# A three-stage attention and mixture-of-experts kernel: a search step's counts moved to ScalarE, a planner with other lengths, and the last expert's chunks in reverse order

## The chip, the cores and the metric

One core of a Trainium2 chip runs the whole kernel in one launch. The metric is device microseconds for that launch, the median of three runs. PE, DVE, ACT, POOL and SP below are the engines TensorE, VectorE, ScalarE, GpSimd and SyncE.

## What is computed

An attention over 2 x 5056 tokens with 256 channels feeds a first mixture of experts, whose result feeds a second one. The change touches the second alone: 8 experts, each takes the 1264 tokens (`cap`) with the largest logits that no earlier entry has taken, and each token is computed by its one expert as two matrix products with a ReLU between.

```python
def _moe2_ref(x, w_gate, w1, w2):
    N, D, E = 10112, 256, 8
    cap = N // E
    logits = x @ w_gate
    ...                       # sorted logits, largest first; token -> expert while the expert has room
    for e in range(E):
        mask = assigned == e
        h = np.maximum(x[mask] @ w1[e], 0.0)     # 256 -> 1024
        out[mask] = h @ w2[e]                    # 1024 -> 256
```

## The kernel before

The attention runs to about 290 us, the first mixture to about 780 us, and the second from there to the end. Only the second stage's instructions stand in another order after the change.

**Routing.** Before expert p can start, its tokens are picked. The threshold is found by a radix search over a 128x688 array of 16-bit keys, first over the high halves (`hk`), then over the low halves (`lk`): `search`, L365 to L404, eight steps each, for seven of the eight experts, so 14 searches and 112 steps. A step compares all keys with three candidates. One of them is always counted on ACT (`sign`, L376, a Sign activation with an accumulated sum), one always on DVE (`count`, L373, a comparison with an accumulated sum); the third goes to ACT in every second step (`i % 2`) and to DVE in the others. `fold` (L384) sums the three counts over the partitions by a tiny matmul on PE, `digit` (L389) and `next_` (L393) on DVE make the next candidates, and the next step starts. ACT and DVE also do the ReLU of the experts (`hh`, L786 on ACT; `hl`, L794, the remainder, on DVE), and PE does their matmuls, so the small instructions of the search are threaded between those.

**Tokens.** `slots` (L602 on) turns the mask into row numbers: `SEL` matmuls (L639), then DVE. `load` (L665) gathers the expert's 1264 rows from DRAM into `xi` with ten indirect DMAs issued by POOL (L682, 128 rows each, the last 112), and copies the token numbers out as `ti` (L686, L687). `split` (L694) transposes the rows on PE (L735) into `xh` (L738, ACT) and `xl` (L743, DVE), chunk by chunk. `CH` is three chunks: 256, 512 and 496 rows (2, 4 and 4 tiles of 128).

**The expert.** `ffn` (L754) runs 20 units per expert. A unit is `F1` (L773, 12 matmuls into `pb`) and, three units later, `F2` (L814, 12 matmuls into `py`). At a chunk's end ACT copies pairs of tiles of `py` to `yo` (L832; L834 and L835 where the last tile is short), and POOL scatters them, one tile at a time, to the output by an indirect DMA (L840). There are two `yo` buffers and one `xi` buffer.

**What sets the order.** `Order` (L215) is a planner that runs when the program is built. Every operation is posted with an assumed duration and its dependencies; the planner repeatedly issues the operation with the earliest start minus a bonus, which the table `BONUS` gives by engine, kind of operation and expert number (0, 1, 2, 3 or more). That fixes the sequence of instructions on each engine; nothing is reordered on the chip.

Of the kernel before, what the change touches and what calls it, by code (L numbers as in the profile page):

```python
# [57 lines left out]
BONUS = {  # L58
    "ACT": (-1.03, -1.15, -1.39, -1.15),
    "ACTC": (-0.13, -0.68, -1.07, -1.07),  # L60
    "ACTH": (-1.73, -0.92, -1.14, -1.04),
    "ACTS": (1.24, -1.09, -0.67, -1.18),
    "ACTW": (-0.91, -1.77, -2.02, -1.86),
    "ACTX": (-0.83, -0.69, -0.38, -0.76),
    "DVE": (2.14, 0.09, 0.17, 0.07),
    "DVEC": (0.18, 0.11, 0.22, 0.09),
    "DVEH": (0.05, 0.14, 0.02, 1.58),
    "DVES": (-0.01, 0.13, 0.03, 0.07),
    "DVEW": (-0.02, 0.05, 0.58, -0.04),
    "DVEX": (4.11, 0.14, 0.02, 1.78),  # L70
    "PE": (-0.22, -0.01, 0.11, 0.1),
    "PEP": (-0.22, -0.14, 0.01, 0.18),
    "PES": (-0.42, 0.06, -0.01, 0.18),
    "PEX": (-0.12, -0.15, 6.41, 0.11),
    "POOL": (1.04, 3.11, 0.41, 1.07),
    "POOLG": (2.72, -1.84, -6.0, 1.07),
    "POOLW": (4.84, 2.33, 1.93, 5.0),
    "SP": (0.14, 3.17, -1.95, 3.19),
}
# [200 lines left out]
def second(ctx, tc, k, l2, code, keyd, ys, w12, w22, out, ident, onesf, trib, ie, rp, r2, late):  # L280
# [84 lines left out]
    def search(x, thr, after, thr_op):  # L365
# [3 lines left out]
        for i in range(ND - 1, -1, -1):  # L369
# [15 lines left out]

            def digit(f=slice(i % 2, i % 2 + 3)):
                j = col("dj", 3)
                s.d = col("dd")
                V.scalar_tensor_tensor(j, s.pe[:, f], 0.0, thr()[:, f], op0=ALU.add, op1=ALU.is_ge, accum_out=s.d)  # L389
# [6 lines left out]

            c3 = A(0.87, lambda c=sign: c(2), *dep, b="C")
            c1 = A(0.87, lambda c=sign: c(3), *dep, b="C") if i % 2 else W(0.86, lambda c=count: c(0), *dep, b="C")
            c2 = W(0.86, lambda c=count: c(1), *dep, b="C")
            ob = W(0.07, base, *dep, c2) if i else None  # L400
# [6 lines left out]
    def route(p_, st, p2):  # L407
# [37 lines left out]
        ont = W(0.07, lambda: above(hf, ss), od, on, b="C")  # L445
        onh = A(0.86, lambda: S.activation(junk2, hk, AF.Sign, bias=hf.nth, accum_out=nh), ont, b="C")
        olk = W(0.85, lambda: V.scalar_tensor_tensor(lk, hk, hf.th, kp[:, 1, :], op0=ALU.is_equal, op1=ALU.mult), oth, b="C")
        z = Slot()
# [76 lines left out]

        onl = A(0.86, nlow, ont, b="C")
        z3 = Slot()
# [137 lines left out]
    def load(st, pv, puts):  # L665
# [23 lines left out]
        for r in range(NR):  # L689
            st.g.append(PL(1.2, lambda r=r: rows(r), st.sis[r], st.g[-1] if r else None, *(pv.xs if pv and not r else []),  # L690
                           *([pv.tok] if pv else [(q, 2.3) for q in puts]), b="G"))
        st.tok = PL(0.3, toks, (st.g[-1], 2.3))

    def split(st, p2, prev):  # L694
# [18 lines left out]
        for j, (h, l, r) in enumerate((("w1h", "w1l", "w1r"), ("w2h", "w2l", "w2r"))):  # L713
            for i in range(4):
                f = (slice(None), slice(2 * i, 2 * i + 2), slice(None)) if j else (slice(None), slice(None), slice(i * 256, i * 256 + 256))
                o = A(0.52, lambda h=h, r=r, f=f, x=(not j and not i): hi(h, r, f, x), (st.w, 7.4 if j else 4.3), wp[0][0] if wp else None,
                      *([p2.last] if p2 else []), b="W")
                o2 = W(0.6, lambda l=l, h=h, r=r, f=f: lo(l, h, r, f), o, b="W")
                wp.append((o, o2))
        st.w1s, st.w2s = wp[:4], wp[4:]  # L720
        st.ws = [q for o in wp for q in o]
        st.xc, st.xs = {}, []
        for ci, (t0, nt, n) in enumerate(CH):
            for c in range(2):
                s, z = State(), Slot()
                ss = slice(t0 * P, t0 * P + n)

                def tr(c=c, s=s, t0=t0, nt=nt, n=n):
                    if t0 == 0 and c == 0:
                        st.xh = pxi.tile([P, 2, NR * P], F32R, name="xh")  # L730
                        st.xl = pxi.tile([P, 2, NR * P], F32R, name="xl")
                    s.pt = qh.tile([P, 512], F32, name="pb")
                    for t in range(nt):
                        m = min(P, n - t * P)
                        T.transpose(s.pt[:, t * P:t * P + m], st.xi[:m, t0 + t, c * P:(c + 1) * P], ident[:m, :m])  # L735
# [4 lines left out]
                def xlo(i, c=c, s=s, t0=t0, nt=nt, n=n):  # L740
# [3 lines left out]

                ot = M(0.107 * nt, tr, (st.g[t0 + nt - 1], 2.3), *([st.xs[-1]] if st.xs else [p2.last] if p2 else []), b="X",
                       take=[("pb", z)])
# [7 lines left out]
    def ffn(st, prev):  # L754
# [46 lines left out]
        def f2(x, y, ci_, t0, nt, n, nch, u):  # L801
# [22 lines left out]
            if u == 8 // nch - 1:  # L824
                for h in range(nt // 2):
# [21 lines left out]
                    for t in range(2):  # L847
                        st.out = PL(1.27, lambda t=2 * h + t, put=put: put(t), oy, st.tok, free=[zy])

        for ci_, (t0, nt, n) in enumerate(CH):  # L850
            nch = 4 // nt
            y = State()
            y.py, y.z = {}, [Slot() for _ in range(nt // 2)]
            for u in range(8 // nch):
                x = State()
                x.zh = Slot()
                units.append((x, y, ci_, t0, nt, n, nch, u))
# [31 lines left out]
    for p_ in range(E):  # L889
# [3 lines left out]
        slots(p_, z, sts[-1] if p_ else None, sts[-2] if p_ > 1 else None)  # L893
        sts.append(z)
        load(z, sts[-2] if p_ else None, () if p_ else puts)
        split(z, sts[-3] if p_ > 1 else None, prev)
# [1179 lines left out]
```

## Time and profile before

| | |
|---|---|
| median of 3 runs | 1435.3 us (1434.08 to 1438.9) |
| the profiled execution's own time | 1436.2 us |
| its span, first to last instruction | 1434.5 us |
| mean granted TensorE clock | 0.951 of full speed |
| PE busy | 1301.4 us, 91% |
| DVE busy | 1094.7 us, 76% |
| ACT busy | 797.6 us, 56% |
| POOL busy | 316.4 us, 22% |

The profile is a record of one execution. Its page gives busy time by engine, the span in 40 equal slices (each digit the busy share in tenths), and the chain of work that ended last. The views used below are the slices and the chain, a table of busy time per stretch of 20 us, the list of waits by releaser, and single instructions in order of time. "another core or an unknown queue" and "remote" mean that the record shows no instruction whose end matches the release; with one core this stands where an engine waited for a signal although the record has the sender done.

### The profile page before, as it was taken

What the parts mean: (1) busy time and instruction counts of PE and PEld (TensorE: products, weight loads), DVE (VectorE), ACT (ScalarE), POOL (GpSimd) and SP (SyncE); (2) the same over time, 40 slices, a digit from 0 to 9 for tenths busy, and PEclk for the clock granted to TensorE, in tenths of its full rate; (3) what the DMA queues carried; (4) which work ended last, traced back from release to release, by engine and by line L of the source; (5) the groups of instructions that cost most, each with busy time, mean ns of one, the idle gap of its engine ahead of it and who ended that gap; (6) DMA issues with size and microseconds to landing.
All of it is one profiled execution on the core that took longest, in us unless ns stands there. A gap on an engine that the chain in (4) does not pass through costs nothing.

```text
span 1434.5 us, 25591 instructions
## 1 busy us (share of the span) xinstructions
PE 1301.4 (91%) x8726; PEld 1169.3 (82%) x8726; DVE 1094.7 (76%) x3720; ACT 797.6 (56%) x1640; POOL 316.4 (22%) x419
## 2 busy tenths in 40 slices
PE   8986858799999999999999987979898999897997
PEld 7886747489988988989987986878888889796897
DVE  8985434698899989798997768989898889685221
ACT  5563424456665666475774657655666666553221
POOL 7634554200000000000000003231423232324312
PEclk9998978799999999999999998989999999998999
DMA  8894531476595959477660981212121212123100
GB/s 292 278 311 150 179 118 61 143 249 192 161 330 170 310 180 293 148 252 248 223 183 16 399 321 50 84 48 78 55 89 45 89 52 85 48 94 107 44 22 30
DMA packets 136226, 223.26 MB, mean 156 GB/s; under 512 B 22016, under 2 KB 99840, under 8 KB 134048
## 3 DMA queue, kind: packets, MB, share of 16 engines
q1 hardware_dynamic: 120256, 186.44, 39.0%
q0 software_dynamic: 11520, 31.73, 6.6%
q10 hardware_dynamic: 4320, 3.46, 0.7%
q8 instruction: 69, 1.13, 0.3%
q14 instruction: 61, 0.50, 0.1%
HBM read 170.18 MB, written 51.41 MB: 154 GB/s over the span
## 4 chain that ended last, share of the span: by engine, by line
PE 71%; DVE 15%; another core or an unknown queue 4%; ACT 4%; issue 3%; DMA 2%; POOL 1%; SPq 0%; ACTq 0%; DVEq 0%; POOLq 0%
PE py L814 15%; PE pb L773 14%; PE pb L1824 12%; PE py L1855 10%; PE pd L2020 4%; PE px L1322 3%; PE ps L1088 2%; PE px L1326 2%; DVE w2l L1793 2%; DVE junk L373 1%; PE pt L1301 1%; DVE hl L1837 1%; PE pt L1770 1%; PE pt L1461 1%
## 5 line engine op out<-in xcount | busy, mean ns | idle before, releaser
L1824 PE MATMUL pb<-xhl,w1h 128*128 128x512 f32 (+1 forms) x800 | 211.1, 351 | 1.7 <-ACT w1h L1787 1.2
L814 PE MATMUL py<-w2l,hh 128*128 128x256 f32 (+1 forms) x640 | 183.9, 287 | 0.0
L814 PE MATMUL py<-w2h,hl 128*128 128x256 f32 (+1 forms) x640 | 183.2, 286 | 0.8 <-issue 0.8
L786 ACT ACTIVATE hh<-pb 128x512 fp32r<-128x512 f32 (+1 forms) x160 | 93.8, 589 | 157.9 <-PE pb L773 112.5
L814 PE MATMUL py<-w2h,hh 128*128 128x256 f32 (+1 forms) x600 | 174.9, 292 | 3.3 <-issue 3.3
L794 DVE SCALAR_TENSOR_TENSOR hl<-pb,hh 128x512 fp32r<-128x512 f32 (+1 forms) x160 | 108.4, 678 | 75.9 <-ACT hh L786 68.6
L1824 PEld LDWEIGHTS pb<-xhl,w1h 128*128 128x128 f32 x800 | 134.1, 190 | 19.2 <-ACT w1h L1787 1.6
L840 POOL DMA_INDIRECT out_dram<-yo,ti x80 | 79.4, 992 | 309.0 <-ACT yo L832 245.2
L1836 ACT ACTIVATE hh<-pb 128x512 fp32r<-128x512 f32 x148 | 88.6, 599 | 104.8 <-PE pb L1824 79.7
L773 PE MATMUL pb<-xh,w1h 128*128 128x256 f32 (+2 forms) x384 | 140.8, 367 | 4.2 <-DVE hl L794 4.2
L1855 PE MATMUL py<-w2h,hh 128*128 128x264 f32 x496 | 143.6, 290 | 0.1
L1855 PE MATMUL py<-w2h,hl 128*128 128x264 f32 x496 | 142.0, 287 | 0.3 <-DVE hl L1837 0.2
L1855 PE MATMUL py<-w2l,hh 128*128 128x264 f32 x496 | 142.2, 287 | 0.0
L773 PE MATMUL pb<-xl,w1h 128*128 128x256 f32 (+2 forms) x384 | 141.1, 368 | 0.4 <-issue 0.2
L773 PE MATMUL pb<-xh,w1l 128*128 128x256 f32 (+2 forms) x384 | 140.1, 365 | 0.0
L1824 PE MATMUL pb<-xhl,w1l 128*128 128x512 f32 (+1 forms) x400 | 138.2, 346 | 0.0
L2034 POOL COPY yo<-xm 128x16 f32<-128x16 f32 x6 | 2.2, 368 | 578.3 <-DVE g L1880 491.6
L814 PEld LDWEIGHTS py<-w2l,hh 128*128 128x128 f32 (+1 forms) x640 | 122.3, 191 | 6.0 <-issue 1.8
L814 PEld LDWEIGHTS py<-w2h,hl 128*128 128x128 f32 (+1 forms) x640 | 122.2, 191 | 2.0 <-issue 0.3
L814 PEld LDWEIGHTS py<-w2h,hh 128*128 128x128 f32 (+1 forms) x600 | 114.7, 191 | 6.2 <-issue 2.4
L1837 DVE SCALAR_TENSOR_TENSOR hl<-pb,hh 128x512 fp32r<-128x512 f32 x148 | 101.3, 684 | 19.1 <-ACT hh L1836 18.3
L682 POOL DMA_INDIRECT xi<-y_scr,si x80 | 80.7, 1009 | 90.1 <-issue 18.6
(521 smaller groups left out, 3714.4 us busy)
## 6 DMA issues: line engine op xcount, KB each, us to landing
w2r<-in_moe_w_dram SPq DMA_DIRECT2D x45, 1024.0 KB
w1r<-in_moe_w_dram SPq DMA_DIRECT2D x41, 1024.0 KB
vt<-in_v_dram SPq DMA_DIRECT2D x18, 512.0 KB
qt<-in_q_dram SPq DMA_DIRECT2D x17, 512.0 KB
kt<-in_k_dram SPq DMA_DIRECT2D x17, 512.0 KB
h_scr<-hh SPq DMA_DIRECT2D x32, 256.0 KB
h_scr<-hl SPq DMA_DIRECT2D x32, 256.0 KB
xi<-xe_scr SPq DMA_DIRECT2D x14, 536.0 KB
```

Of the source, the lines that this page charges most:

```text
L682: G.indirect_dma_start(out=st.xi[:n, r, :], out_offset=None, in_=ys, in_offset=bass.IndirectOffsetOnAxis(ap=st.si[:n, r:r + 1], axis=0))
L773: T.matmul(x.pb[:, ci, :n], a[:, c, fc * P:fc * P + P], b_[:, c, xs_], start=(c == 0 and i == 0), stop=(c == 1 and i == 2))
L786: S.activation(x.hh[:, :, :n], x.pb[:, :, :n], AF.Relu)
L794: V.scalar_tensor_tensor(x.hl[f], x.pb[f], 0.0, x.hh[f].bitcast(F32), op0=ALU.max, op1=ALU.subtract)
L814: T.matmul(py[:m_, t % 2, :], a[:, ci, t * P:t * P + m_], b_[:, fc, :], start=False, stop=(fc == 7 and i == 2 and t % 2 == 1))
L840: s_ = G.indirect_dma_start(out=out, out_offset=bass.IndirectOffsetOnAxis(ap=st.ti[:m_, t0 + t:t0 + t + 1], axis=0), in_=q.yo[:m_, t % 2, ...
L1322: T.matmul(w.px[:np_, :D + 2 * E], h.vh[:, cc, tt, :np_], r[:, cc, :], start=(i == 0), stop=False)
L1824: T.matmul(o, a[:, c, ws], xhl[:, c, h, :], start=(i == 0), stop=(i == 5))
L1836: S.activation(hh, pb, AF.Relu)
L1837: V.scalar_tensor_tensor(hl, pb, 0.0, hh.bitcast(F32), op0=ALU.max, op1=ALU.subtract)
L1855: T.matmul(py[t][:, :width], a[:, ci, ts_], b_[:, fc, :width], start=(fc == 0 and i == 0), stop=(fc == 7 and i == 2))
L2020: T.matmul(py[t][:, :D], a[:, ts_], b_[:, fc, :D], start=(fc == 0 and i == 0), stop=(fc == 7 and i == 2))
```

## The change

Three edits. First, in `search` the third candidate goes to ACT where `i % 4` is not zero, six steps of eight in place of four. Second, the planner's assumed lengths: a sign 1.0 us (was 0.87), a count 0.9 (0.86), a gather's issue 1.4 (1.2) and its landing 3.0 (2.3), a scatter's issue 1.42 (1.27), the casts of the weights 5.0 and 8.0 us after their load is issued (4.3 and 7.4), and another `BONUS` table. Third, the last expert runs its chunks in reverse: 496, 512, 256 rows.

```diff
 BONUS = {
-    "ACTS": (1.24, -1.09, -0.67, -1.18),
+    "ACTS": (0.14, -0.62, 1.75, -0.54),
...
-    "POOLG": (2.72, -1.84, -6.0, 1.07),
+    "POOLG": (2.41, -2.03, -5.16, -0.42),
...
-            def digit(f=slice(i % 2, i % 2 + 3)):
+            def digit(f=slice(i % 4 > 0, (i % 4 > 0) + 3)):
...
-            c3 = A(0.87, lambda c=sign: c(2), *dep, b="C")
-            c1 = A(0.87, lambda c=sign: c(3), *dep, b="C") if i % 2 else W(0.86, lambda c=count: c(0), *dep, b="C")
-            c2 = W(0.86, lambda c=count: c(1), *dep, b="C")
+            c3 = A(1.0, lambda c=sign: c(2), *dep, b="C")
+            c1 = A(1.0, lambda c=sign: c(3), *dep, b="C") if i % 4 else W(0.9, lambda c=count: c(0), *dep, b="C")
+            c2 = W(0.9, lambda c=count: c(1), *dep, b="C")
...
-            st.g.append(PL(1.2, lambda r=r: rows(r), st.sis[r], st.g[-1] if r else None, *(pv.xs if pv and not r else []),
+            st.g.append(PL(1.4, lambda r=r: rows(r), st.sis[r], st.g[-1] if r else None, *(pv.xs if pv and not r else []),
...
-        st.tok = PL(0.3, toks, (st.g[-1], 2.3))
+        st.tok = PL(0.4, toks, (st.g[-1], 3.0))
...
-                o = A(0.52, lambda h=h, r=r, f=f, x=(not j and not i): hi(h, r, f, x), (st.w, 7.4 if j else 4.3), wp[0][0] if wp else None,
+                o = A(0.52, lambda h=h, r=r, f=f, x=(not j and not i): hi(h, r, f, x), (st.w, 8.0 if j else 5.0), wp[0][0] if wp else None,
...
-        for ci, (t0, nt, n) in enumerate(CH):
+        for ci, (t0, nt, n) in st.ch:
...
-                    if t0 == 0 and c == 0:
+                    if ci == st.ch[0][0] and c == 0:
...
-                ot = M(0.107 * nt, tr, (st.g[t0 + nt - 1], 2.3), *([st.xs[-1]] if st.xs else [p2.last] if p2 else []), b="X",
+                ot = M(0.107 * nt, tr, (st.g[t0 + nt - 1], 3.0), *([st.xs[-1]] if st.xs else [p2.last] if p2 else []), b="X",
...
-                        st.out = PL(1.27, lambda t=2 * h + t, put=put: put(t), oy, st.tok, free=[zy])
+                        st.out = PL(1.42, lambda t=2 * h + t, put=put: put(t), oy, st.tok, free=[zy])
...
-        for ci_, (t0, nt, n) in enumerate(CH):
+        for ci_, (t0, nt, n) in st.ch:
...
+        z.ch = list(enumerate(CH))[::-1 if p_ == E - 1 else 1]
```

The order moves in many places of the second stage. Three of them follow.

POOL, the gathers (L682) of expert 6 and the scatters (L840, each with a small MEMSET ahead of it) of expert 5 around them, before:

```order
L682 DMA xi<-y_scr,si 128x260 x7
L839 MEMSET gap 128x1
L840 DMA out_dram<-yo,ti 10112x256
L682 DMA xi<-y_scr,si 128x260
L839 MEMSET gap 128x1
L840 DMA out_dram<-yo,ti 10112x256
L839 MEMSET gap 128x1
L840 DMA out_dram<-yo,ti 10112x256
L839 MEMSET gap 128x1
L840 DMA out_dram<-yo,ti 10112x256
L682 DMA xi<-y_scr,si 128x260
L682 DMA xi<-y_scr,si 112x260
```

The same place after:

```order
L682 DMA xi<-y_scr,si 128x260 x9
L682 DMA xi<-y_scr,si 112x260
L839 MEMSET gap 128x1
L840 DMA out_dram<-yo,ti 10112x256
L839 MEMSET gap 128x1
L840 DMA out_dram<-yo,ti 10112x256
```

The ten gathers of expert 6 stand in one piece, and the scatters that stood between them stand behind them. For expert 5 the order was the same as for expert 6 and becomes the same; for expert 7 one scatter stood after the fourth and one after the fifth gather, and now none stands between. Experts 1 and 3 had their ten gathers in one piece before and have it still; expert 4 had it, and now has one scatter after its second gather; expert 2 had four scatters ahead of its last gather, and has them after its seventh.

ACT, one search over the high halves, the fifth of seven, for expert 4 (`cnt` is the counts of a step, two buffers in turn, so a row "x2" on one `cnt` is two candidates of one step; `dr` and `w1h` belong to the next tokens and weights), before:

```order
L376 ACTIVATE junk_10962,cnt_10964<-hk,k_kk 128x688 x2
L629 CAST dr_10968<-pc 128x87
L786 ACTIVATE hh<-pb 128x496
L376 ACTIVATE junk_10962,cnt_10963<-hk,cand 128x688
L832 COPY yo<-py 128x512 x2
L786 ACTIVATE hh<-pb 128x496
L376 ACTIVATE junk_10962,cnt_10964<-hk,cand 128x688 x2
L707 CAST w1h<-w1r 128x2x256
L786 ACTIVATE hh<-pb 128x496
L376 ACTIVATE junk_10962,cnt_10963<-hk,cand 128x688
```

The same search after:

```order
L376 ACTIVATE junk_10962,cnt_10964<-hk,k_kk 128x688 x2
L786 ACTIVATE hh<-pb 128x496
L707 CAST w1h<-w1r 128x2x256
L376 ACTIVATE junk_10962,cnt_10963<-hk,cand 128x688 x2
L786 ACTIVATE hh<-pb 128x496
L832 COPY yo<-py 128x512
L376 ACTIVATE junk_10962,cnt_10964<-hk,cand 128x688 x2
L832 COPY yo<-py 128x512
L786 ACTIVATE hh<-pb 128x496
L738 CAST xh<-pb 128x256
L376 ACTIVATE junk_10962,cnt_10963<-hk,cand 128x688
```

The second step, which counted one candidate on ACT, counts two; the fourth still counts one.

ACT, the end of the program, the last expert's ReLUs (`hh`) and output copies (`yo`), before:

```order
L786 ACTIVATE hh<-pb 128x512 x7
L832 COPY yo<-py 128x512
L786 ACTIVATE hh<-pb 128x512 x5
L786 ACTIVATE hh<-pb 128x496 x3
L832 COPY yo<-py 128x512 x2
L786 ACTIVATE hh<-pb 128x496 x5
L832 COPY yo<-py 128x512
L834 COPY yo<-py 128x256
L835 COPY yo<-py 112x256
```

The same place after:

```order
L786 ACTIVATE hh<-pb 128x496 x8
L786 ACTIVATE hh<-pb 128x512 x3
L832 COPY yo<-py 128x512
L834 COPY yo<-py 128x256
L835 COPY yo<-py 112x256
L786 ACTIVATE hh<-pb 128x512 x8
L832 COPY yo<-py 128x512 x2
L786 ACTIVATE hh<-pb 128x512
L832 COPY yo<-py 128x512
```

Behind the last ReLU three copies with four tiles stood, and now one with two tiles stands there.

## Rows read from the trace of the kernel before

**Rows 1.** the page: engines and granted clock in 40 slices, then the chain by engine

```profile
PE   8986858799999999999999987979898999897997
...
PEclk9998978799999999999999998989999999998999
...
PE 71%; DVE 15%; another core or an unknown queue 4%; ACT 4%; issue 3%; DMA 2%; POOL 1%; SPq 0%; ACTq 0%; DVEq 0%; POOLq 0%
```

**Rows 2.** stretches: length, busy PE, PEld, DVE, ACT, POOL; clock, DMA share, GB/s

```profile
880.00:900.00 20.00, 17.73 (x113) 15.47 (x114) 19.60 (x70) 13.68 (x29) 3.38 (x8) 1.00 0.08 26
...
920.00:940.00 20.00, 14.96 (x109) 12.36 (x107) 16.29 (x59) 13.56 (x29) 9.39 (x12) 0.98 0.42 137
...
1020.00:1040.00 20.00, 18.91 (x140) 17.71 (x141) 19.25 (x71) 15.58 (x33) 5.79 (x11) 1.00 0.09 32
...
1080.00:1100.00 20.00, 17.91 (x143) 17.33 (x144) 17.73 (x49) 15.57 (x33) 11.09 (x19) 1.00 0.20 65
...
1140.00:1160.00 20.00, 20.00 (x159) 19.09 (x158) 18.53 (x60) 15.46 (x34) 12.18 (x15) 1.00 0.29 81
...
1220.00:1240.00 20.00, 13.29 (x80) 11.70 (x81) 10.16 (x27) 7.55 (x16) 10.89 (x17) 0.83 0.23 71
...
1280.00:1300.00 20.00, 18.09 (x139) 16.40 (x137) 13.79 (x39) 8.25 (x18) 11.71 (x15) 0.94 0.72 250
1300.00:1320.00 20.00, 13.29 (x84) 11.99 (x83) 12.43 (x28) 9.01 (x17) 3.26 (x5) 0.72 0.08 26
1320.00:1340.00 20.00, 16.53 (x105) 14.47 (x104) 6.02 (x12) 5.29 (x11) 12.15 (x17) 1.00 0.28 80
```

**Rows 3.** the chain from 780 us: start, us, what held it

```profile
935.35 2.69 another core or an unknown queue
...
1014.96 2.90 another core or an unknown queue
...
1084.90 1.77 another core or an unknown queue
...
1226.79 7.15 another core or an unknown queue
...
1292.72 3.71 another core or an unknown queue
1298.26 7.38 another core or an unknown queue
...
1328.09 9.23 another core or an unknown queue
```

**Rows 4.** POOL in order of time, expert 5's gathers: start, us, idle before

```profile
1212.46 1.42 POOL L682 DMA_INDIRECT xi<-y_scr,si  x1 [8.50 <-PE pe L384]
...
1223.64 0.99 POOL L840 DMA_INDIRECT out_dram<-yo,ti  x1 [0.19 <-issue]
...
1231.30 0.95 POOL L682 DMA_INDIRECT xi<-y_scr,si  x1 [0.31 <-issue]
```

**Rows 5.** lines 373 and 376: durations min/median/max in ns

```profile
L373 DVE TENSOR_SCALAR_CACHE_REDUCE junk<-hk,cand x77: 911/924/931, 791.1 to 1241.6; 128x688 bf16<-128x688 uint16 x77
L373 DVE DVE_READ_ACCUMULATOR junk<-hk,cand x77: 75/82/85, 791.9 to 1242.4; 128x1 fp32r x77
...
L376 ACT ACTIVATE junk<-hk,cand x70: 857/869/882, 791.1 to 1240.3; 128x688 bf16<-128x688 uint16 x70
L376 ACT ACTIVATION_READ_ACCUMULATOR junk<-hk,cand x70: 185/187/206, 791.9 to 1241.1; 128x1 fp32r x70
```

**Rows 6.** waits of the second stage: us in total, times, longest

```profile
PE pe L384 <- ACT junk L376: 13.2, 9, 3.3
```

**Rows 7.** the end, in order of time

```profile
1425.84 0.28 PE L814 MATMUL py<-w2h,hl 128*112 128x256 f32 x1
...
1426.31 0.96 POOL L840 DMA_INDIRECT out_dram<-yo,ti  x1 [13.48 <-ACT yo L832]
...
1430.10 0.94 POOL L840 DMA_INDIRECT out_dram<-yo,ti  x1 [0.19 <-issue]
```

## What the change will do to the time

> **What bounds the kernel now.** I read the 40 slices first, then the chain, then the second stage in stretches of 20 us, then single instructions of the poor stretches. The slices say that PE is the bound: nines nearly everywhere in the second half [rows 1], where the change works, and the chain is PE for 71% of the span. A time is to be had only where PE is not at nine, or is at nine with a lower clock. The stretches show where that is. In the middle of an expert PE is busy 20.00 of 20 us, even through the whole gather of expert 4 (1140 to 1160). Around the gathers of the last three experts it is not: expert 5 has 13.29 of 20 (1220 to 1240), expert 6 has 18.09 and 13.29 (1280 to 1320), expert 7 has 16.53 (1320 to 1340) [rows 2]. Together that is 6.71 + 1.91 + 6.71 + 3.47 = 18.8 us without a matmul, and in two of the stretches the granted clock is 0.83 and 0.72, so that part of them ran at 1.2 in place of 2.4 GHz. Earlier experts lose less: expert 1 lost 5.04 (920 to 940), expert 3 lost 2.09 (1080 to 1100), expert 4 nothing.
>
> The chain says the same in another way. Behind 780 us it names seven stretches in which the engine that was last had no sender in the record: 2.69, 2.90 and 1.77 us for experts 1, 2 and 3, then 7.15, 3.71, 7.38 and 9.23, which is 27.5 us, inside the gathers of experts 5, 6 and 7 [rows 3]. What differs there is the order on POOL. Expert 5's ten gathers began at 1212.46, the last at 1231.30, with scatters such as that of 1223.64 between them [rows 4]; experts 1, 3 and 4 had ten in a piece. A tile's transpose waits for its gather, and PE runs its queue in order: a gather that comes late holds not only the new expert's transposes but every matmul behind them.
>
> **Part 1, the gathers in one piece.** For experts 5 and 6 the new order takes four scatters from between the gathers, for expert 7 two. An issue of this kind takes (1430.10 - 1426.31) / 3 = 1.26 us [rows 7], so the last gather starts 5.1 us sooner (2.5 in expert 7), and expert 5's window falls from 18.8 us to about 13.7. On PE the first F1 of experts 5, 6 and 7 also stands later against the older work, because the planner now reckons 1.4 us per gather and 3.0 for its landing. The upper bound of the gain takes the chain's 27.5 us and leaves each of the three a clean expert's share, (2.69 + 1.77 + 0) / 3 = 1.5: 23 us. The middle value takes the time without a matmul, 18.8 us, and leaves the clean mean of (5.04 + 2.09 + 0) / 3 = 2.4 each: 11.6 us. The other end is 0. I take **-15**, between the two ways of counting and nearer to the idle time, since the chain also counts time in which PE's records are busy, while the low clock, which the idle time doesn't count, goes with the stall. The scatters that are put behind the gathers cost nothing as long as the two `yo` buffers come free in time; a chunk of four tiles is 8 units' worth of work, and two buffers wait at most for the ten gathers, 12.6 us.
>
> The trace has the low clock only behind stalls: 1.00 in the stretch 1140 to 1160 without a gap, 0.83 and 0.72 in those with 6.7 us of them [rows 2]. The Trainium skill, "TensorE: Matmul & The Clock Gate", section "HAM oscillation — how this bites in real kernels", says that waits between bursts of matmuls put the clock back to half, so that a wait is paid a second time by what follows it. The trace agrees with 0.72. By that rule the gain would be the idle time and the clock's share, nearer to the upper bound.
>
> **Part 2, the third candidate on ACT.** In each of 14 searches two of eight steps change: 28 candidates. A count takes 0.924 + 0.082 = 1.006 us of DVE, a sign 0.869 + 0.187 = 1.056 us of ACT [rows 5]. DVE loses 28 x 1.006 = 28.2 us of work, 4 us per expert, and ACT gets 28 x 1.056 = 29.6. The length of a step hardly changes: two counts in a row (2.01) were its longest part where two candidates were DVE's, two signs (2.11) are it now, 0.1 us x 28 = 2.8 us of search, which has no room to matter unless the search itself is last. On the path is only what DVE held PE up: DVE is full in 880 to 900 (19.60 of 20) and 1020 to 1040 (19.25), where PE lost 2.27 and 1.09 us [rows 2]. So at best -3.4; I take **-3**. ACT stays under 16 of 20 us in the transitions shown (15.57, 15.58) [rows 2], so its average has room; its queue is in order, though, and a sign of 0.87 us ahead of a ReLU can delay an F2. What is to be seen of that today is PE waiting for a fold whose sign was late: 13.2 us in 9 places, 1.47 each [rows 6]. The planner took two signs for 1.74 us, 0.37 less than they last, and now takes 2.0, 0.11 less, so each fold is put later and waits less. With 84 two-sign steps in place of 56 the wait would rise by half, +6.6; with the truer lengths it could fall by as much. I take **0**, with -6 and +13 as the ends (+13 is worked out under the second rival).
>
> The Trainium skill, "ScalarE: Activation LUTs", section "Rules for kernel authors", speaks against this part: simple arithmetic belongs on VectorE, up to about three times faster. Here the two differ by 5% (1.006 against 1.056), so the rule's gain is not there; by it the move would cost ACT much more than DVE gets back.
>
> **Part 3, the short chunk last.** Behind the last matmul, which ends at 1425.84 + 0.28 = 1426.1, four scatters follow from 1426.31, the last at 1430.10, and the span ends 4.4 us later [rows 7]. With two tiles at the end there are two scatters: 2 x 1.26 = 2.5 us sooner. The first of them no longer overlaps PE's last matmuls, since its copy now waits for the very last one: 0.5 us back. **-2**; the scatters of the chunk before it have the last chunk's four units of matmuls as cover.
>
> **The sum.** 1436.2 (the profiled execution, 0.9 above the median) - 15 - 3 + 0 - 2 = 1416.2; against the median 1435.3 that is **1415**. The first stages keep their order and their time.
>
> **Rivals.** First: the stalls belong to ten gathers as such, not to what stands between them. For it: expert 1 lost 5.04 us with ten in a piece, about as much as expert 5; the late experts also load weights (DMA at 250 GB/s in 1280 to 1300, the place of expert 6's gathers [rows 2]), which the change doesn't move. Against it: expert 4 lost nothing. Then only parts 2 and 3 are left: 1435.3 - 3 - 2 = 1430.
>
> Second, slower: the sign becomes the end of the step. The place is the fold on PE, behind which all F1 and F2 queue; the price is 1.47 us for each fold that is reached before its sign is read out. If 9 of the 28 new two-sign steps wait so, that is +13, and a search that ends later makes the mask, the row numbers and the gathers late, so that part 1 brings nothing: 1435.3 + 13 - 3 - 2 = 1443. With part 1 gone it decides from the fourth such step on (4 x 1.47 = 5.9 against 5); with part 1 in place only from the fourteenth. For it: PE waits for late signs already. Against it: the longer assumed sign, by which each fold is put later.
>
> Third: the last expert gives its gain back. Its first chunk is now of tiles 6 to 9, so no F1 can start before the last of ten gathers, where two were enough: 8 x 1.26 = 10.1 us later, against three units of F2 in hand (36 matmuls, 4.5 us at the 159 in 20 us of the stretch 1140 to 1160 [rows 2]). Its 5 us of part 1 go, and 10.1 - 4.5 = 5.6 are added: 1426.
>
> Fourth: the low clock goes with the stalls and the upper bound of part 1 is reached, and folds wait less: 1435.3 - 23 - 3.4 - 2.5 - 1 = 1405.
>
> **How the numbers follow.** My forecast, 1408 to 1420, has 42%; the third rival's 1426 has 14%, the fourth 8%, the first 16%, the second, with what else could make it slower, 20%. The predicted time is 1415. What a measurement can tell from no change is 0.3%, 4.3 us: the limits are 1431.0 and 1439.6. Faster takes the forecast, the third, the fourth and half of the first: 72%. Within takes the other half and the mild end of the second: 11%. Slower: 17%. The range leaves out the second rival's middle and upper end and the far end of the fourth: 1403 to 1438.
>
> **What would show it.** Right: the three stretches of the chain without a sender in experts 5 to 7 are gone or under 3 us each, the stretches there show PE above 18 of 20 with the clock at 1.00, the gathers of experts 5 to 7 span about 14 us, DVE's full stretches fall under 19, and two scatters stand behind the last matmul. Wrong on part 1: stalls of 7 us stay with gathers in one piece. Wrong on part 2: the fold's waits for a sign grow past 13.2 us, or new waits of `hl` and F2 for a late ReLU appear. Wrong on part 3: a wait of PE at the start of the last expert that is longer than 9.23 us.

## The result and the profile after

The changed kernel took 1451.0 us (median of 4 runs, 1443.7 to 1454.8) against 1434.7 us of the kernel before (4 runs): a ratio of 1.0102, interval 1.0057 to 1.0146. It is slower by 1.0%, where 1415 us, 1.4% faster, was predicted.

The jobs (a job is a set of runs made together on one chip) fell into two kinds, whatever the kernel and not tied to a chip: in *late* jobs, as in the one of the prediction, the kernel before took 1434 to 1438 us and some of PE's results reached the other engines late, and in *prompt* jobs it took 1344 to 1349 us and no such result is in any trace. Kernels are compared with the kernel before of their own job, except where the difference between the kinds is the subject.

The page of the changed kernel, its slices of PE and clock, and its chain by engine (the answer to [rows 1]):

```profile
PE   8988767699999999999999979798869889898998
...
PEclk9999878799999999999999989899999989999999
...
PE 70%; DVE 14%; issue 4%; ACT 4%; another core or an unknown queue 4%; DMA 4%; POOL 1%; SPq 0%; POOLq 0%; ACTq 0%; DVEq 0%
```

The weak slices have moved forward: sixes and sevens stand now where experts 0 to 4 change over. Stretches of 20 us of the changed kernel (length, busy PE, PEld, DVE, ACT, POOL, clock, DMA share, GB/s), the answer to [rows 2]:

```profile
880.00:900.00 20.00, 19.86 (x131) 17.95 (x131) 15.87 (x61) 15.67 (x34) 6.47 (x11) 1.00 0.13 40
...
920.00:940.00 20.00, 10.92 (x63) 10.00 (x62) 11.02 (x32) 9.79 (x21) 5.63 (x9) 0.74 0.15 43
...
1080.00:1100.00 20.00, 13.74 (x88) 13.20 (x89) 13.63 (x42) 13.43 (x27) 2.07 (x4) 0.74 0.05 19
...
1140.00:1160.00 20.00, 13.42 (x89) 11.38 (x87) 8.63 (x31) 8.79 (x20) 13.91 (x18) 0.90 0.42 126
1160.00:1180.00 20.00, 15.82 (x102) 14.62 (x103) 14.64 (x46) 14.02 (x30) 1.01 (x5) 0.76 0.02 7
...
1220.00:1240.00 20.00, 17.70 (x117) 14.76 (x116) 13.55 (x48) 12.46 (x27) 13.94 (x17) 1.00 0.45 138
1240.00:1260.00 20.00, 16.79 (x120) 15.90 (x119) 15.98 (x46) 14.83 (x32) 4.85 (x12) 0.91 0.09 33
...
1300.00:1320.00 20.00, 14.25 (x101) 13.43 (x100) 11.38 (x31) 5.91 (x13) 9.92 (x11) 0.83 0.50 158
1320.00:1340.00 20.00, 19.90 (x144) 18.29 (x142) 14.12 (x28) 11.07 (x22) 13.15 (x17) 1.00 0.31 95
1340.00:1360.00 20.00, 17.23 (x104) 15.59 (x105) 6.57 (x11) 6.32 (x12) 4.21 (x10) 0.91 0.09 31
```

The second stage as a whole, from its first matmul of one group (the marks of the last table under Experiments) to the end, in the same columns, before and then after:

```profile
791.90:1434.50 642.60, 580.71 (x4026) 531.50 (x4024) 461.92 (x1548) 353.32 (x728) 173.99 (x260) 0.96 0.28 96
...
781.50:1448.70 667.20, 590.52 (x4026) 539.69 (x4024) 442.51 (x1489) 378.85 (x782) 169.37 (x260) 0.94 0.26 92
```

PE does the same 4026 matmuls. The stage is 24.6 us longer: PE waits 14.8 us more (76.7 against 61.9), and its records are 9.8 us longer, at a mean granted clock of 0.94 against 0.96. The part ahead of the mark, which the change leaves alone, was 10.4 us shorter in this one profile, so the spans differ by 14.2 us only. Expert 1 (920 to 940) lost 9.1 us, experts 3 and 4 lost 6.3 and 6.6 + 4.2 us in the stretches shown, and the clock fell to 0.74 to 0.90 with them. In all stretches from 900 to 1180, which hold experts 1 to 4, PE waits 42.5 us where it waited 19.2; from 1220 to 1360, which hold experts 5 to 7, it waits 14.8 where it waited 18.8. DVE is relieved, but by 19.4 us and not by the 28.2 worked out: the records of a count, of its read and of the next instruction overlap, so adding their durations says too much. The stretch 880 to 900 has DVE at 15.87 of 20 where it was at 19.60. The chain's stretches without a sender in the record (the answer to [rows 3]: start, us):

```profile
921.30 6.63 another core or an unknown queue
...
1020.68 3.19 another core or an unknown queue
...
1072.89 10.60 another core or an unknown queue
...
1150.41 12.22 another core or an unknown queue
...
1308.74 5.59 another core or an unknown queue
```

They are 38.2 us where they were 34.8, and have gone from experts 5 and 7 to experts 1, 3 and 4. What such a stretch is shows in the single instructions of expert 4's (start, us, engine, line, in brackets the idle time ahead and its releaser):

```profile
1149.49 0.27 PE L384 MATMUL pe<-cnt,k_blk 128*128 128x4 f32 x1 [0.34 <-issue]
...
1152.71 0.58 ACT L786 ACTIVATE hh<-pb 128x496 fp32r<-128x496 f32 x1 [3.28 <-PE pb L773]
...
1155.02 0.28 PE L814 MATMUL py<-w2h,hl 128*112 128x256 f32 x1
...
1162.65 0.16 DVE L389 SCALAR_TENSOR_TENSOR dj<-pe,k_thr 128x3 f32<-128x3 f32 x1 [12.24 <-remote]
...
1163.81 0.75 PE L773 MATMUL pb<-xh,w1h 128*128 128x496 f32 x1 [8.52 <-DVE hl L794]
```

PE's fold of a search step stands in the record at 1149.49, and PE goes on through matmuls queued behind it until 1155.3. DVE, which needs that fold, gets it at 1162.65, 12.9 us after it ended. Not every result is late: ACT's ReLU at 1152.71 starts 0.9 us behind the matmuls that it reads. Once it has the fold, DVE makes `hl`, and PE, out of work for 8.5 us, starts again. Among the ten gathers of expert 4 a single scatter stood, after the second; those of experts 1 and 3, with stretches of 6.63 and 10.60 us, stood in one piece. The waits of the second stage (who waits, for whom, us in total, times, longest), DVE's for a fold before and after, then the answer to [rows 6]:

```profile
DVE dj L389 <- remote: 14.6, 4, 7.2
...
DVE dj L389 <- remote: 32.6, 4, 12.2
...
PE pe L384 <- ACT junk L376: 17.4, 9, 7.9
```

The longest of these nine waits for a sign, 7.9 us, follows a late result: DVE got a fold late at 928.66, so the next step's sign was late too, and the next fold waited for it.

```profile
928.66 0.16 DVE L389 SCALAR_TENSOR_TENSOR dj<-pe,k_thr 128x3 f32<-128x3 f32 x1 [6.50 <-remote]
...
931.38 0.37 PE L384 MATMUL pe<-cnt,k_blk 128*128 128x4 f32 x1 [7.92 <-ACT junk L376]
```

The other eight make 9.5 us. Of the nine waits of before, 13.2 us in all, the longest, 3.3 us, follows a late result too, and the other eight make 9.9.

### The profile page after: what moved, and what is told of

Its sections match the earlier page's. It is cut to its first block, busy times and chain, and to the rows that moved or that the text cites. A ratio compares the mean times of both kernels' runs of the same rounds, so it can differ in the third digit from the quotient of the medians.

```text
span 1448.7 us, 25584 instructions
## 1 busy us (share of the span) xinstructions
PE 1303.2 (90%) x8726; PEld 1170.8 (81%) x8726; DVE 1075.6 (74%) x3664; ACT 825.3 (57%) x1696; POOL 312.9 (22%) x419
## 4 chain that ended last, share of the span: by engine, by line
PE 70%; DVE 14%; issue 4%; ACT 4%; another core or an unknown queue 4%; DMA 4%; POOL 1%; SPq 0%; POOLq 0%; ACTq 0%; DVEq 0%
PE pb L773 14%; PE py L814 14%; PE pb L1826 13%; PE py L1857 10%; PE px L1324 3%; PE pd L2022 3%; PE px L1328 2%; PE pt L1303 1%; ACT junk L376 1%; PE pb L735 1%; DVE junk L373 1%; DVE w2l L1795 1%; PE pt L1772 1%; PE ps L1090 1%
## 5 line engine op out<-in xcount | busy, mean ns | idle before, releaser
L814 PE MATMUL py<-w2h,hl 128*128 128x256 f32 (+1 forms) x640 | 188.3, 294 | 2.2 <-issue 1.1
L814 PE MATMUL py<-w2l,hh 128*128 128x256 f32 (+1 forms) x640 | 187.2, 292 | 1.2 <-issue 1.1
L794 DVE SCALAR_TENSOR_TENSOR hl<-pb,hh 128x512 fp32r<-128x512 f32 (+1 forms) x160 | 108.4, 679 | 76.7 <-ACT hh L786 64.1
L773 PE MATMUL pb<-xh,w1h 128*128 128x496 f32 (+2 forms) x384 | 142.2, 370 | 9.7 <-DVE hl L794 9.6
L840 POOL DMA_INDIRECT out_dram<-yo,ti x80 | 78.7, 984 | 323.3 <-ACT yo L832 176.8
L773 PE MATMUL pb<-xl,w1h 128*128 128x496 f32 (+2 forms) x384 | 141.5, 369 | 0.8 <-DVE xl L743 0.8
L773 PE MATMUL pb<-xh,w1l 128*128 128x496 f32 (+2 forms) x384 | 140.9, 367 | 0.0
L814 PEld LDWEIGHTS py<-w2h,hl 128*128 128x128 f32 (+1 forms) x640 | 125.4, 196 | 3.3 <-DVE hl L794 1.1
L814 PEld LDWEIGHTS py<-w2h,hh 128*128 128x128 f32 (+1 forms) x600 | 117.9, 197 | 5.5 <-issue 1.2
L682 POOL DMA_INDIRECT xi<-y_scr,si x80 | 78.4, 981 | 111.6 <-PE pc L639 34.5
```

The lines of the kernel that those rows point to most:

```text
L682: G.indirect_dma_start(out=st.xi[:n, r, :], out_offset=None, in_=ys, in_offset=bass.IndirectOffsetOnAxis(ap=st.si[:n, r:r + 1], axis=0))
L773: T.matmul(x.pb[:, ci, :n], a[:, c, fc * P:fc * P + P], b_[:, c, xs_], start=(c == 0 and i == 0), stop=(c == 1 and i == 2))
L794: V.scalar_tensor_tensor(x.hl[f], x.pb[f], 0.0, x.hh[f].bitcast(F32), op0=ALU.max, op1=ALU.subtract)
L814: T.matmul(py[:m_, t % 2, :], a[:, ci, t * P:t * P + m_], b_[:, fc, :], start=False, stop=(fc == 7 and i == 2 and t % 2 == 1))
L840: s_ = G.indirect_dma_start(out=out, out_offset=bass.IndirectOffsetOnAxis(ap=st.ti[:m_, t0 + t:t0 + t + 1], axis=0), in_=q.yo[:m_, t % 2, ...
```

## Experiments

Three readings stood against each other. *Theory S*: the added signs end the search steps later, and PE waits for them at the fold. *Theory L*: PE's results are late while POOL gathers, and an order loses by how much of it depends on PE in those stretches. And the prediction's own: scatters between gathers make the stalls, so that gathers in one piece gain.

**The parts one by one, in late jobs.** `a_sign` is the kernel before with the search rule alone:

```diff
-            def digit(f=slice(i % 2, i % 2 + 3)):
+            def digit(f=slice(i % 4 > 0, (i % 4 > 0) + 3)):
...
-... if i % 2 else W(0.86, lambda c=count: c(0), *dep, b="C")
+... if i % 4 else W(0.86, lambda c=count: c(0), *dep, b="C")
```

> The kernel before with the search rule alone: two candidates on ScalarE in six of eight steps, old planner lengths and bonuses, last expert's chunks in the old order. Theory S (the added signs end the steps later, 28 signs of 1.06 us): slower than before by 8 to 16 us, 1443 to 1451, with PE's waits for a sign at the fold grown from 13 to about 25 us. Theory L (PE's results reach the other engines late while POOL gathers rows, and each order loses by how much depends on PE in that window): between 1425 and 1445, and the difference to before sits in stretches in which POOL gathers, not in the sign waits. Part 2 of the prediction: 1432.

Measured: 1460.0 against 1437.9 us, ratio 1.0172 (1.0126 to 1.0218). The search rule under the old plan costs 1.7%, more than the whole change. Its waits (releaser, us in total, times, longest):

```profile
PE pe L384 <- ACT junk L376: 42.2, 20, 8.5
ACT hh L786 <- remote: 18.3, 2, 9.4
DVE dj L389 <- remote: 15.3, 2, 9.4
```

PE's waits for a sign at the fold are 42.2 us where they were 13.2 [rows 6], more than either theory expected, as is the time. That is the second rival's mechanism, but not it alone: the two longest waits, 8.5 and 8.0 us, end 2.5 us behind a result of PE that came late to DVE. In this order the gathers of experts 4 to 7 stand in one piece; the sum of waits on a sender not in the record is smaller than before, but not gone.

`b_oldrule` is the changed kernel with `i % 2` in those two places:

> The changed kernel with the old search rule (two candidates on ScalarE in four of eight steps); new planner lengths, bonuses and the last expert in reverse. Theory S: the loss goes, 1420 to 1435. Theory L: the loss stays about as it is with the change, 1440 to 1455, in the gather windows. In this order the gathers of experts 4 to 7 stand in one piece, so part 1 of the prediction expects 1418.

Measured: 1443.3 against 1437.9 us, ratio 1.0045 (1.0017 to 1.0073). The plan without the rule does not make the kernel faster either, with all gathers of experts 4 to 7 in one piece: part 1 of the prediction, tried without the rule, gives no gain. The rule adds 8 us to it by the ratios, and 12.5 us against `c_norev`, which follows.

`c_norev` is the changed kernel with the last expert in the old order (`z.ch = list(enumerate(CH))`), `d_rev` the kernel before with the reversal alone (the lines of the diff with `ch` in them).

> The changed kernel with the last expert's chunks in the old order. The reversal was priced at -2 us at the end of the program: by that alone 1453 against 1451. By the third rival (the reversed first chunk waits for all ten gathers) it is faster than the changed kernel, about 1446. Theory L: the planner's order also moves a little elsewhere (two scatters stand between gathers again), so anything from 1440 to 1458.

> The kernel before with the last expert's chunks in reverse and nothing else; in this order the gathers of experts 5 and 6 still have scatters between them. By the tail alone 1433; by the third rival 1438 to 1440, with a longer wait of PE at the start of the last expert.

Measured: `c_norev` 1455.8 us, 1.0124 (1.0079 to 1.0169); `d_rev` 1434.4 us, 0.9990 (0.9961 to 1.0019). Both were run again in another late job.

> The changed kernel with the last expert's chunks in the old order. Without late results (before 1342 to 1352): the changed kernel is at 0.994 of before; two scatters more behind the last matmul cost 2 us, so 0.995 to 0.997. By the third rival (the reversed first chunk waits for all ten gathers) it is faster than the changed kernel, 0.990 or less. With late results: 1.010 to 1.015.

> The kernel before with the last expert in reverse. Two scatters fewer behind the last matmul: 0.998 to 0.999 of before on either kind of chip. By the third rival: 1.001 to 1.004.

Measured: 1451.5 us, 1.0103 (1.0054 to 1.0152), and 1436.4 us, 0.9997 (0.9968 to 1.0026). The reversal is worth nothing that a run can tell, and no run shows the 5.6 us that the third rival put on it. Its 2 us are seen in the traces alone (below).

**Is the lateness the order's?** The changed kernel was run again beside two kernels that test the gathers. In `f_sync` each gather is a plain copy of 128 rows that stand together, issued by SyncE; in `f_pool` POOL issues it:

```diff
-            G.indirect_dma_start(out=st.xi[:n, r, :], out_offset=None, in_=ys,
-                                 in_offset=bass.IndirectOffsetOnAxis(ap=st.si[:n, r:r + 1], axis=0))
+            r0 = sts.index(st) * CAP + r * P
+            nc.sync.dma_start(st.xi[:n, r, :], ys[r0:r0 + n, :])
...
-            G.tensor_copy(st.ti[:, :NR - 1], st.xi[:, :NR - 1, D + 1])
-            G.tensor_copy(st.ti[:NL, NR - 1:], st.xi[:NL, NR - 1:, D + 1])
+            G.iota(st.ti, pattern=[[P, NR]], base=sts.index(st) * CAP, channel_multiplier=1)
```

> The changed kernel once more, as the base for the two kernels beside it on the same chip. If the lateness of PE's results is a property of the order, the same four or five stretches without a sender (experts 1, 3, 4 above all, 6 to 12 us each) stand in it again and the idle time of PE from 780 us is near 70 us; if it is chance, they are elsewhere.

> The changed kernel with its gathers replaced: each of the ten blocks of an expert's rows is a plain copy of 128 rows that stand together, issued by SyncE on a hardware queue, and the token numbers are counted up instead of read (so the tokens are shared out by position, not by the search; the search, the selection and all matmuls run as before). Theory L (PE's results are late because POOL gathers by indirect DMA): the waits on a sender not in the record go from about 60 us to under 10, the clock stays at 1.00 through the transitions, 1405 to 1425. Theory S (the signs): the late stretches stay, 1440 to 1455.

> As f_sync, but the plain copies are issued by POOL in the place of the indirect ones. If it is the indirect addressing or the row-wise packets, the late stretches go, 1405 to 1425; if it is any transfer that POOL issues, they stay, 1440 to 1455.

These kernels leave out the choice of rows: they fetch other rows than the search picks, so they are a test and no remedy, and the copies also do not wait for the search. The job was prompt: the kernel before took 1349.1 us, the changed one 1336.8, `f_sync` 1338.7, `f_pool` 1336.5. The same program that lost 38 us in stretches without a sender has none here, so they are not a property of the order alone. Where nothing is late, how the rows are fetched gains nothing. `f_sync2`, `f_sync3` and `f_pool2` met prompt jobs as well (1344.0, 1341.8 and 1343.2 us, where the kernel before took 1346.0, 1344.6 and 1345.4). `f_sync2` was 5.5 us slower than the changed kernel beside it, outside the 3 us expected, and `f_pool2` 1 us above its range; they tell no more of the lateness.

> The changed kernel with plain copies by SyncE in place of the gathers, tokens shared out by position. On a chip with late results this is the test that the first run of it could not make: if indirect gathers by POOL make PE's results late, the waits on a sender not in the record in the second stage fall from about 60 us to under 10 and the time by 30 us or more against the changed kernel beside it; if the lateness has nothing to do with the gathers, the time stays within 8 us of it. Without late results: equal to the changed kernel within 3 us.

> The changed kernel with plain copies by SyncE in place of the gathers, tokens shared out by position. With late results: if the indirect gathers by POOL make them, the second stage is shorter than the changed kernel's 671 us by 30 us or more and the time 1390 to 1420, while the first stage keeps its 279 us; if not, 1443 to 1455. Without late results: 1336 to 1345.

> The changed kernel with the plain copies issued by POOL in the place of the indirect gathers, tokens shared out by position. With late results: near 1395, as with SyncE's copies, if the indirect addressing makes them; 1440 to 1455 if any transfer that POOL issues does. Without late results: 1334 to 1342, which tells nothing new.

`f_sync4` met a late job, the one of `c_norev2` and `d_rev2`:

> The changed kernel with plain copies by SyncE in place of the gathers, tokens shared out by position. With late results: if the indirect gathers make them, the second stage is under 640 us against the changed kernel's 671 and the time 1390 to 1420; if not, 1443 to 1455. Without late results: within 6 us of 1338.

Measured: 1395.4 us in one run, where the kernel before took 1436.1 and the changed kernel, but for the last expert's order, 1451.5. Waits of `c_norev2`, then of `f_sync4`, from their late matmuls on:

```profile
DVE dj L389 <- remote: 39.1, 6, 12.2
ACT hh L786 <- remote: 21.8, 3, 7.5
ACT xh L738 <- remote: 13.2, 3, 6.7
```

```profile
PE pe L384 <- ACT junk L376: 9.0, 7, 2.4
```

Of waits on a sender not in the record (`remote`) `f_sync4` has none: without POOL's gathers no result of PE comes late in this stage, although the scatters are still POOL's. So in this stage the gathers, as POOL issues them, make the lateness.

They are not the only transfers that do. In the attention stage, which has no gathers, POOL issues 80 indirect scatters (`xe_scr`) in series of eight and sixteen, and there `f_sync4` has 36.9 us of waits on a sender not in the record, all within such series or up to 3 us behind them. The two largest groups of these waits are:

```profile
ACT xs L1332 <- remote: 16.2, 5, 5.3
ACT vh L1308 <- remote: 8.0, 1, 8.0
```

The first mixture, in which POOL issues no transfer, has none in any job; the second stage of `f_sync4`, whose scatters come at most four at a time, has none either. What nearly all late stretches share is thus a longer series of indirect transfers, gathers or scatters, that POOL issues without a pause; no experiment varies the length of such a series by itself. In prompt jobs series as long have no late result.

Whether it is the indirect addressing or that POOL issues the transfers is open: `f_pool` met no late job. The Trainium skill, "DMA: Bandwidth & Descriptors", section "SWDGE vs HWDGE vs iDMA", says that POOL writes the descriptors of its transfers into rings in on-chip memory, which SyncE's transfers don't use. No run here shows whether that is the reason.

**The change without late results.** `after3` is the changed kernel again, `before_p` the kernel before, for its trace in a prompt job.

> The changed kernel again, in rounds. On a chip on which PE's results come late in the transitions (before near 1437): 1445 to 1455, slower than before by 0.6 to 1.4%. On one on which they do not (before near 1349): 1333 to 1341, faster by 0.6 to 1.2%.

> The kernel before, unchanged, for its trace on this chip. Without late results: 1342 to 1352, no wait on a sender not in the record in the second stage, PE's idle time from the first late matmul on about 30 us, of it the sign waits at the fold some 10 us. With them: 1430 to 1445, with 30 to 50 us of such waits.

Measured: 1338.5 against 1346.0 us, ratio 0.9936 (0.9909 to 0.9963), so faster by 0.6%; `before_p` 1344.5. Waits and the end of `before_p`:

```profile
PE pe L384 <- ACT junk L376: 5.8, 5, 2.2
PE pb L735 <- DMA xi<-y_scr,si: 6.5, 5, 2.4
```

```profile
1334.11 0.28 PE L814 MATMUL py<-w2h,hl 128*112 128x256 f32 x1
...
1338.38 0.95 POOL L840 DMA_INDIRECT out_dram<-yo,ti  x1 [0.19 <-issue]
```

and of `after3`:

```profile
PE pe L384 <- ACT junk L376: 6.5, 7, 2.1
PE pb L735 <- DMA xi<-y_scr,si: 2.7, 3, 1.0
```

```profile
1327.67 0.28 PE L814 MATMUL py<-w2h,hl 128*128 128x256 f32 x1
...
1330.15 0.96 POOL L840 DMA_INDIRECT out_dram<-yo,ti  x1 [0.19 <-issue]
```

Here the parts can be seen apart. PE waits 3.8 us less for gathers, never more than 1.0 us for one; the fold waits hardly change; and from the end of PE's last matmul to the end of the span it is 1342.8 - 1334.4 = 8.4 us before and 1334.4 - 1328.0 = 6.4 after, the 2 us of part 3.

**The parts in prompt jobs.** `b_oldrule2` and `a_sign2` are `b_oldrule` and `a_sign` again. `g_len` is `a_sign` with a sign planned at its measured length: `A(1.06, ...)` in place of `A(0.87, ...)` in both places.

> The changed kernel with the old search rule, again. If late results come: 1437 to 1449 as before. If they do not: this tells what the search rule is worth there. Theory S (a sign on ScalarE costs the search more than a count on DVE): faster than the changed kernel by 2 to 8 us. Part 2 of the prediction (DVE relieved by 28 us of work): slower than it by 2 to 4 us.

> The kernel before with the new search rule alone, again. With late results: 1458 to 1464. Without: if the wait for the sign at the fold is its cost (42 us of waits on the first chip against 13), it stays slower than before by 15 us or more there too; if late results made the cost, it comes within 5 us of before.

> The kernel before with the new search rule (two candidates on ScalarE in six of eight steps), as a_sign, but the planner reckons 1.06 us for a sign, what it lasts, in place of 0.87. Theory S in its narrower form (the folds are planned too early): PE's waits for a sign at the fold fall from 42 us to under 20 and the time from 1460 to 1440 or less. If the sign itself is the end of the step whatever the plan says: the waits stay over 30 us, 1455 to 1462.

Measured: `b_oldrule2` 1368.1 against 1346.0 us, 1.0154 (1.0116 to 1.0193); `a_sign2` 1366.0 us in the same job; `g_len` 1393.8 against 1349.1 us, 1.0326 (1.0280 to 1.0372). The rule alone costs 20 us here too, where nothing is late; the plan alone (lengths, bonuses and the reversal) costs 22 us; the two together gain 7.5. `b_oldrule2` missed both expectations: it is 30 us slower than the changed kernel beside it. And a true length for the sign in the old plan makes it worse by far, not better: the narrower form of theory S falls. The waits at the fold in `a_sign2`, `g_len` and `b_oldrule2`, in this order:

```profile
PE pe L384 <- ACT junk L376: 16.1, 12, 2.6
```

```profile
PE pe L384 <- ACT junk L376: 19.5, 15, 2.6
```

```profile
PE pe L384 <- ACT junk L376: 13.5, 11, 2.9
...
PE pe L384 <- DVE junk L373: 12.0, 9, 2.5
```

`after3` has 6.5. The plan and the rule fit each other only: with the old rule under the new plan the folds wait 25.5 us, nearly half of it for counts on DVE, and with the new rule under the old bonuses 16.1 and 19.5 us for signs. These waits are not the whole of the losses: by the ratios to the kernel before of its job `g_len` takes some 24 us more than `a_sign2`, and it waits 3.4 us more for signs. Which of the new lengths and bonuses matter was not tried one by one.

**What the lateness costs each order.** From the first matmul of one group of the late stage (`pd<-w2h,w1r`, the same in all kernels) to the end of the span, in us, from one profile each:

The marks are the first starts of that group and the spans; for the changed kernel in a late and in a prompt job the group's rows are (durations in ns, first and last start):

```profile
L2022 PE MATMUL pd<-w2h,w1r x80: 276/279/390, 781.5 to 838.2; 128*128 128x256 f32 x80
```

```profile
L2022 PE MATMUL pd<-w2h,w1r x80: 275/279/387, 739.4 to 796.1; 128*128 128x256 f32 x80
```

| kernel | late job | prompt job | difference |
|---|---|---|---|
| before (`before_p` in the prompt job) | 1434.5 - 791.9 = 642.6 | 1342.8 - 737.0 = 605.8 | 36.8 |
| changed (`after3` in the prompt job) | 1448.7 - 781.5 = 667.2 | 1334.4 - 739.4 = 595.0 | 72.2 |
| rule alone (`a_sign`, `a_sign2`) | 1457.1 - 781.6 = 675.5 | 1364.0 - 741.0 = 623.0 | 52.5 |
| old rule (`b_oldrule`, `b_oldrule2`) | 1444.6 - 788.5 = 656.1 | 1366.5 - 740.9 = 625.6 | 30.5 |
| plain copies (`f_sync4`, `f_sync3`) | 1393.7 - 787.0 = 606.7 | 1340.1 - 743.1 = 597.0 | 9.7 |

The changed order is the best of the first four in prompt jobs by 11 us and loses twice as much as the one before, 72 against 37 us, when PE's results are late. Single profiles of nearly the same kernels differ: in late jobs the stage is 641.9 and 652.6 us in `d_rev` and `d_rev2`, and 669.7 and 662.9 in `c_norev` and `c_norev2`. By these the losses are 36 to 47 us and 68 to 76.

## Why the prediction was wrong

**What bounds the kernel.** That PE is the bound and that the time lies around the gathers was right. The step that failed is the reading of [rows 3], on which part 1 rests: the stretches without a sender were put down to scatters between the gathers, because the three experts with scatters had the long ones. They are results of PE that arrive late, they come with POOL's gathers as such, and in which expert they come differs by order: with the gathers of experts 4 to 7 in one piece but for one scatter, PE waited 14.8 us more in the stage. The trace of before had said it, though no row shows it: the fold, the ReLU and the transposes' copies waited for a sender not in the record while PE's own records ran on, and part 1 itself notes that PE's records are busy in that time. A gather that holds PE's queue would have stopped PE's records at the transpose.

**Part 1, -15.** Wrong in its cause, in its size and in what it left out. Experts 5 to 7 waited 14.8 us, only 4.0 less than the 18.8 of before, and experts 1 to 4, for which the prediction had no change, 42.5 - 19.2 = 23.3 us more. The clean expert's share was also too low: it took one stretch of 20 us for each expert and left out the one beside it, in which PE lost 2.6, 2.6 and 1.9 us for experts 1, 3 and 4, so that it was near 4.7 and not 2.4:

```profile
940.00:960.00 20.00, 17.41 (x105) 16.72 (x106) 16.88 (x54) 12.15 (x27) 7.66 (x13) 0.68 0.15 46
...
1060.00:1080.00 20.00, 17.44 (x125) 15.42 (x121) 16.54 (x60) 13.39 (x29) 8.13 (x10) 1.00 0.42 139
...
1160.00:1180.00 20.00, 18.07 (x120) 16.15 (x118) 16.89 (x57) 12.38 (x27) 5.04 (x12) 1.00 0.09 33
```

The prediction's own sign against part 1 came: stalls of 7 us with gathers in one piece, 10.60 us in expert 3. In prompt jobs PE's waits for gathers fell by 3.8 us, so even there -15 was four times too much.

**Part 2, -3 and 0.** The 28 moved candidates came; DVE's busy time fell by 19.4 us where 28.2 were worked out. What that relief is worth by itself no run shows. That the sign can end the step was the second rival, and it is part of what the rule does by itself: some 10 us of fold waits in a prompt job (16.1 against 5.8), and 29 in the late `a_sign`, of which 16.5 follow late results. With the new plan nothing of it is left: 6.5 against 5.8 us in prompt jobs, and in the late one 9.5 against 9.9, leaving out the waits that follow late results. So the second rival had the direction of the result right and its cause wrong. The term 0 held by luck: the reason given was the truer length of a sign, and that length alone does not lower the waits (19.5 us in `g_len`). It held only for rule and plan together. I priced the bonus table at nothing, and the new plan gains 27.5 us with the new rule (1338.5 against 1366.0) and costs 22 with the old one.

**Part 3, -2.** Right in the traces, 2.0 us, and below what runs can tell. The third rival's 10 us of waiting for the last gather did not come: in `after3` PE waits for no gather longer than 1.0 us.

**The first rival** had the right place, stalls that come with ten gathers as such, and the wrong bound: it let them stay as they were. None of the cases let them grow; the only slower one, the second rival, stood for another cause, and the range was cut at 1438, below its 1443.

**What stays open.** Why the changed order is hit harder by late results: with the new plan the rule raises the loss from 30.5 to 72.2 us, with the old plan from 36.8 to 52.5, and the new plan without the rule does not raise it, so the two edits act together. What the traces show is another kind of late result: DVE's waits for a fold went from 14.6 to 32.6 us, and ACT's for what the ReLU reads fell from 24.2 to 2.3. Also open is what makes a job late; what runs ahead of the second stage, which the change leaves alone, is longer in late jobs as well, and has the attention stage's late results: the group of matmuls with which the table above begins comes at 782 to 792 us there and at 737 to 743 in prompt ones.

## What to carry to other kernels

Where an engine waits on a sender that the record shows as done long ago, look at which transfers run in those stretches before blaming the order of instructions, and try the same stretch with the transfers issued in another way: here that took away what no reordering did, in one run of a kernel that fetched other rows. A plan fitted to one set of costs belongs to them: half of such a change can lose more than the whole gains. And measure a change of order in more than one job: this one is 1.0% slower in one kind and 0.6% faster in the other.

## What was not expected of the hardware

Some of PE's results reached DVE and ACT up to 12.9 us late while PE's records ran on. In late jobs this came with longer series of indirect transfers issued by POOL: ten gathers of an expert in the second stage, eight or sixteen scatters in the attention stage, and not with series of at most four scatters. Replacing the gathers by copies from SyncE's queue took 56 us off the kernel there (1395.4 against 1451.5) and nothing in prompt jobs (2 to 6 us slower than the changed kernel beside it). The same program differed by 113 us between jobs (1451.0 and 1338.5).
